# Splitting float64 weights in place, two chunks at a time, without GpSimd

## The chip, the core and the metric

The kernel runs on one core of one Trainium2 chip, as a single launch. The metric is the device time in microseconds, the median of several runs. The engines of a core are TensorE (PE in the rows; its weight loads are PEld), VectorE (DVE), ScalarE (ACT), GpSimd (POOL) and SyncE (SP), whose queue issues all the loads and stores of this kernel.

## What is computed

Three blocks follow one another: a small two-way attention between 512 tokens and 32 state rows per head, a gated feed-forward block with a convolution over three positions, and a second feed-forward block with a squared ReLU and a gate.

```python
# x: (8, 8, 512, 64), state: (8, 8, 32, 64), float32
a = softmax(scale * x @ state.T);  xread = a @ state
a2 = softmax(scale * state @ x.T); sread = a2 @ x
x = concatenate([xread, sread], axis=2)        # per batch: 544 tokens of 512 features
h = maximum(x @ w_in, 0)                       # w_in: 512 x 1024
conv = sum over k of conv_w[k] * h[token + k - 1]
x = (h * sigmoid(conv)) @ w_out                # w_out: 1024 x 512
prev = x of the token before
k = maximum((mu_k * x + (1 - mu_k) * prev) @ w_k, 0)     # w_k: 512 x 1024
r = sigmoid((mu_r * x + (1 - mu_r) * prev) @ w_r)        # w_r: 512 x 512
out = r * ((k * k) @ w_v)                      # w_v: 1024 x 512
```

The five weight matrices and conv_w come as float64.

## The kernel before

Every float32 product runs as three float32r passes: an operand is split into hi, its upper 12 significant bits, and lo, the rest, and hi*hi, hi*lo and lo*hi are accumulated (`mm3`, L112 to L114). So every weight has to be split on the chip before it is used.

A matrix comes in chunks of 128 x 512 entries: 8 of w_in, 8 of w_out, 8 of w_k, 8 of w_v and 4 of w_r, 36 in all. `Weights.load` loads a chunk twice, as two transfers of 512 KB: `raw` holds the 64 bits of each entry as two words, `mid` the same bits shifted by 16, so that one word has the lower part of the mantissa. `Weights.split` makes hi and lo of a chunk: ScalarE takes the magnitude (L156) and the sign (L162) of the upper words into the working tiles `val` and `exp`; VectorE clamps the exponent (L158) and shifts it to its place (L159); GpSimd multiplies by the sign, which is hi (L163); VectorE takes the exponent of hi (L164) and the lower bits of `mid` (L167). The low product is one VectorE instruction (L171) for w_in and w_v, and a ScalarE copy (L173) with a GpSimd product (L174) for w_out, w_k and w_r. `raw` and `mid` have three slots each, `val` and `exp` two each. The slots of `raw` serve the tiles of `pair_m` as well.

Phase 1 has nine tiles: eight batches of 512 positions, and one that gathers the positions whose convolution needs the state's read. A tile has eight slots of 128 hidden features. In a slot TensorE makes h (hps), ScalarE and VectorE make the convolution (L444, L446) and the gate (L454, L456), the gated h is split (L462, L464), and TensorE accumulates the product with w_out (acc). In the first three tiles the low part of the gated h (L464) is GpSimd's, and in the first tile the gating (L456) too. The read of the attention is not formed: h = relu(a m) with m = state w_in, made per batch (`Attention.m`) or for two batches together (`pair_m`). Phase 2 runs over tiles of 384 and then 512 tokens: the mixes with the previous token (L534 to L542), k (kps), its square and split (L557 to L571), r (rps) and the product with w_v.

The order of work is a list of half-slots. `at_half(k, ...)` says at which half-slot a step is written down and with what priority; a scheduler then lays out each engine's fixed order by priority and its own estimate of times. `weight_at(w, need, at)` places a chunk's load and split by the half-slot that needs it. w_in and w_out are split during the first tile, w_k, w_v and w_r during the last tiles of phase 1 and the first of phase 2.

Of the kernel before, what the change touches and what calls it, by code (L numbers as in the profile page):

```python
# [23 lines left out]
# Half-slots of a tile at which the next batch's attention starts, and from a batch's first  # L24
# half-slot those at which the parts of state w_in are made.
# [5 lines left out]
def tile_kernel(  # L31
# [76 lines left out]
    def mm3(ps, lhs, rhs, start, stop):  # L108
        """lhs, rhs: lists over the contraction of (hi, lo)."""
        last = len(lhs) - 1  # L110
        for k, ((lh, ll), (rh, rl)) in enumerate(zip(lhs, rhs)):
            nc.tensor.matmul(ps, lh, rh, start=start and k == 0, stop=False)  # L112
            nc.tensor.matmul(ps, lh, rl, start=False, stop=False)  # L113
            nc.tensor.matmul(ps, ll, rh, start=False, stop=stop and k == last)  # L114

    # ---------------------------------------------------------------- weights
    class Weights:
        """A [P, n] array in DRAM as its (hi, lo); float64 comes as its bits, in an integer type."""

        def __init__(self, src, n, pool, tag=""):  # L120
            self.src, self.n, self.pool, self.tag = src, n, pool, tag
            self.wide = src.dtype != F32

        def tile(self, shape, dt, name, bufs):
            return self.pool.tile(shape, dt, tag=name + self.tag, name=name, bufs=1 if self.tag else bufs)

        def load(self):
            if not self.wide:
                self.raw = self.tile([P, self.n], F32, "raw", 3)
                nc.sync.dma_start(out=self.raw, in_=self.src)  # L130
# [5 lines left out]
            nc.sync.dma_start(  # L136
                out=self.mid.rearrange("p n two -> p (n two)").bitcast(U16)[:, :n],
                in_=self.src.bitcast(U16)[:, 1:1 + n],
            )

        def split(self, w, eng):
            """w[:, 0] + w[:, 1] is the value, to float32's precision or better.

            float64: the exponent is clamped to float32's range and moved to its place; with the sign
            and the upper 11 bits of the mantissa it is hi. The next 25 bits, as a number, times the
            power of two is lo; the load that is off by 16 bits has them in one word."""
            hi, lo = w[:, 0], w[:, 1]
            if not self.wide:
                nc.scalar.activation(hi, self.raw, AF.Copy)
                eng.tensor_tensor(lo, self.raw, hi.bitcast(F32), op=ALU.subtract)  # L150
# [11 lines left out]
            nc.scalar.activation(ef, high.bitcast(F32), AF.Sign)  # L162
            nc.gpsimd.tensor_tensor(hi, vf, ef, op=ALU.mult)  # L163
# [3 lines left out]
            nc.vector.tensor_scalar(  # L167
                v, self.mid[:, :, 0], scalar1=0x1FFFFFF, scalar2=None, op0=ALU.bitwise_and
            )
# [8 lines left out]
    def weight(src, key, tag, pool, eng, many=1):  # L178
        """The two steps in which chunk `key` of a matrix gets ready."""
        r = Weights(src, N, stg)  # L180

        def split():
            name, k = key
            if k % many == 0:
                W[name, "group", k // many] = pool.tile(
                    [P, 2, many, N], F32R, tag=f"{tag}{k // many}", name=f"{name}{k}"
                )
            W[key] = W[name, "group", k // many][:, :, k % many]
            r.split(W[key], eng)

        return r.load, split

    # ---------------------------------------------------------------- attention
# [28 lines left out]
    def pair_m(b, q, g):  # L222
        """state w_in of both batches, for the q-th pair of column blocks and the heads of group g.

        Its rows come out by batch and then head; the copies between partitions put each batch's
        rows together."""
# [7 lines left out]
        r = stg.tile([P, 2, 2, 2 * P], F32R, tag="raw", name="m", bufs=3)  # L234
# [7 lines left out]
    class Attention:  # L242
# [9 lines left out]
        def state(self):  # L252
            """The batch's state^T, with the heads of a group side by side."""
# [9 lines left out]
        def m(self, q, f0, n):  # L263
            """state w_in for the column blocks f0.. f0 + n of the q-th pair of them."""
# [545 lines left out]
```

## Time and profile before

| | before |
|---|---|
| median of 3 runs | 915.64 us (915.46 to 915.88) |
| span of the profiled execution, first to last instruction | 912.2 us |
| TensorE busy (4440 matmuls) | 858.1 us, 94% |
| VectorE busy | 589.2 us, 65% |
| ScalarE busy | 543.4 us, 60% |
| GpSimd busy | 195.1 us, 21% |
| mean granted TensorE clock | 0.976 of full speed |

The time of the profiled execution itself isn't listed beside its span; the runs lie 3.4 us above the span. The shares are means over the whole span; the stages differ, and the rows below are taken by stretch. In the rows a duration in the groups is a mean in ns, and "idle before" is the time that the engine waited in front of the group.

### The profile page before, as it was taken

The page shows a single profiled execution, that of the slowest core. Times are in us where ns is not written, and L with a number is a line of the kernel's source. Part 1 is how long each engine was busy: PE and PEld are TensorE (multiplying, and loading weights), DVE is VectorE, ACT ScalarE, POOL GpSimd, SP SyncE. Part 2 cuts the span into 40 slices and gives each one's busy share as a digit, 9 for nine tenths or more (in the row PEclk, how much of TensorE's full clock was granted, in tenths as well). Part 3 has the DMA queues.
Part 4 walks back from the last instruction along what each step waited for, and adds up shares of the span by engine and source line. Part 5 has one row for each costly group of instructions (what it writes and reads, how often), then busy time and mean ns, then how long its engine had stood idle before and what let it go on. Part 6 is the DMA issues. An engine that isn't in the chain of part 4 may idle for free.

```text
span 912.2 us, 12185 instructions
## 1 busy us (share of the span) xinstructions
PE 858.1 (94%) x4440; PEld 693.0 (76%) x4440; DVE 589.2 (65%) x1001; ACT 543.4 (60%) x985; POOL 195.1 (21%) x280
## 2 busy tenths in 40 slices
PE   4877999999999998998879999999999999999997
PEld 2565677778778876788758888888888888888886
DVE  6999998799889978999895542533435234232221
ACT  4666686678558758777666753645546354553431
POOL 3567754242111113436530000000000000000000
PEclk7778999999999999999999999999999999999999
DMA  9944335534443437426832011111011110011010
GB/s 346 323 160 153 124 131 139 155 111 133 158 126 115 116 94 233 163 83 225 287 108 81 19 29 46 47 47 44 4 47 47 47 47 17 30 35 47 0 47 35
DMA packets 50843, 95.77 MB, mean 105 GB/s; under 512 B 9056, under 2 KB 31072, under 8 KB 48736
## 3 DMA queue, kind: packets, MB, share of 16 engines
q1 hardware_dynamic: 50784, 95.00, 32.1%
q8 instruction: 35, 0.57, 0.3%
q14 instruction: 24, 0.20, 0.1%
HBM read 64.54 MB, written 17.86 MB: 90 GB/s over the span
## 4 chain that ended last, share of the span: by engine, by line
PE 66%; DVE 22%; ACT 4%; DMA 3%; issue 2%; SPq 1%; POOL 1%; DVEq 0%; ACTq 0%; POOLq 0%
PE acc L113 10%; PE acc L114 10%; PE acc L112 10%; PE kps L112 6%; PE kps L113 6%; PE kps L114 6%; DVE cacc L446 5%; PE rps L113 3%; PE rps L114 3%; PE rps L112 3%; DVE val L167 2%; DVE exp L164 2%; DVE val L159 2%; PE hps L112 2%; DVE g L456 2%
## 5 line engine op out<-in xcount | busy, mean ns | idle before, releaser
L571 DVE TENSOR_TENSOR ks<-k,ks 128x512 fp32r<-128x512 f32 (+1 forms) x72 | 48.6, 676 | 116.7 <-ACT ks L570 116.1
L446 DVE SCALAR_TENSOR_TENSOR cacc<-hb,vcol,cacc 128x512 f32<-128x512 f32 (+1 forms) x144 | 112.2, 790 | 4.1 <-ACT cacc L444 3.7
L112 PE MATMUL kps<-xk,k 128*128 128x512 f32 (+1 forms) x288 | 110.6, 384 | 3.7 <-ACT xk L541 3.0
L113 PE MATMUL acc<-gs,out 128*128 128x512 f32 (+1 forms) x288 | 111.4, 387 | 1.8 <-DVE gs L464 1.8
L114 PE MATMUL acc<-gs,out 128*128 128x512 f32 (+1 forms) x288 | 108.0, 386 | 2.8 <-POOL out L174 2.8
L113 PE MATMUL kps<-xk,k 128*128 128x512 f32 (+1 forms) x288 | 110.1, 382 | 0.0
L114 PE MATMUL kps<-xk,k 128*128 128x512 f32 (+1 forms) x288 | 110.0, 382 | 0.0
L112 PE MATMUL acc<-v,ks 128*128 128x512 f32 x272 | 105.9, 393 | 2.8 <-ACT ks L570 1.4
L113 PE MATMUL acc<-v,ks 128*128 128x512 f32 x272 | 105.9, 390 | 0.4 <-DVE v L171 0.4
L114 PE MATMUL acc<-v,ks 128*128 128x512 f32 x272 | 105.1, 392 | 0.0
L112 PE MATMUL acc<-gs,out 128*128 128x512 f32 (+1 forms) x288 | 100.0, 388 | 3.0 <-POOL out L163 2.2
L536 DVE SCALAR_TENSOR_TENSOR mix<-yt,muc,mix 128x384 f32<-128x384 f32 (+7 forms) x128 | 66.6, 542 | 49.4 <-ACT mix L534 48.8
L534 ACT ACTIVATE mix<-yt,om 128x384 f32<-128x384 f32 (+7 forms) x128 | 61.4, 516 | 39.0 <-DMA yt<-y 20.3
L570 ACT ACTIVATE ks<-k 128x512 fp32r<-128x512 f32 (+1 forms) x72 | 43.4, 604 | 67.1 <-PE acc L114 66.9
L557 ACT ACTIVATE k<-kps 128x512 f32<-128x512 f32 (+1 forms) x72 | 40.7, 567 | 48.4 <-PE kps L114 48.0
L113 PEld LDWEIGHTS acc<-gs,out 128*128 128x128 f32 x288 | 55.1, 191 | 15.1 <-DVE gs L464 2.5
L112 PEld LDWEIGHTS acc<-gs,out 128*128 128x128 f32 x288 | 55.0, 192 | 15.1 <-POOL out L163 3.0
L114 PEld LDWEIGHTS acc<-gs,out 128*128 128x128 f32 x288 | 54.6, 191 | 14.4 <-POOL out L174 2.9
L112 PEld LDWEIGHTS kps<-xk,k 128*128 128x128 f32 x288 | 54.2, 188 | 14.9 <-ACT xk L541 3.4
L113 PEld LDWEIGHTS kps<-xk,k 128*128 128x128 f32 x288 | 54.4, 189 | 10.2
L114 PEld LDWEIGHTS kps<-xk,k 128*128 128x128 f32 x288 | 54.3, 189 | 10.2
L112 PEld LDWEIGHTS acc<-v,ks 128*128 128x128 f32 x272 | 50.9, 188 | 14.3 <-POOL v L163 2.0
(134 smaller groups left out, 1882.5 us busy)
## 6 DMA issues: line engine op xcount, KB each, us to landing
out<-r SPq DMA_DIRECT2D x34, 256.0 KB, 2.1
xT<-x_t SPq DMA_DIRECT2D x32, 256.0 KB, 4.1
xn<-x_n SPq DMA_DIRECT2D x8, 1024.0 KB, 5.9
y<-yo SPq DMA_DIRECT2D x8, 1024.0 KB, 4.3
me<-m SPq DMA_DIRECT2D x48, 128.0 KB, 2.4
m_odd<-m SPq DMA_DIRECT2D x48, 128.0 KB, 2.4
raw<-w_in SPq DMA_DIRECT2D x8, 512.0 KB, 5.8
raw<-w_out SPq DMA_DIRECT2D x8, 512.0 KB, 4.8
```

The costliest lines, as they stand in the source:

```text
L112: nc.tensor.matmul(ps, lh, rh, start=start and k == 0, stop=False)
L113: nc.tensor.matmul(ps, lh, rl, start=False, stop=False)
L114: nc.tensor.matmul(ps, ll, rh, start=False, stop=stop and k == last)
L159: nc.vector.tensor_scalar(v, v, scalar1=3, scalar2=0xFFFFF000, op0=ALU.logical_shift_left, op1=ALU.bitwise_and)
L164: nc.vector.tensor_scalar(e, hi.bitcast(U32), scalar1=0xFF800000, scalar2=None, op0=ALU.bitwise_and)
L167: nc.vector.tensor_scalar(v, self.mid[:, :, 0], scalar1=0x1FFFFFF, scalar2=None, op0=ALU.bitwise_and)
L446: nc.vector.scalar_tensor_tensor(a[:, :n], hb[:, k:k + n], w[k], a[:, :n], op0=ALU.mult, op1=ALU.add)
L534: nc.scalar.activation(tmp[:, o:o + m], y[:, c, q - 1:q - 1 + m], AF.Copy, scale=om[:, i:i + 1])
L536: nc.vector.scalar_tensor_tensor(tmp[:, o:o + m], y[:, c, q:q + m], muc[:, i:i + 1], tmp[:, o:o + m], op0=ALU.mult, op1=ALU.add,)
L557: nc.scalar.activation(k[:, :n], s["p"][:, :n], AF.Relu)
L570: nc.scalar.activation(ks[:, 0, :n], s["k2"][:, :n], AF.Copy)
L571: nc.vector.tensor_tensor(ks[:, 1, :n], s["k2"][:, :n], ks[:, 0, :n].bitcast(F32), op=ALU.subtract)
```

## The change

A `Weights` object now stands for `many` chunks of a matrix (two for all five matrices, one for conv_w), loaded by one pair of transfers for each chunk into one slot for all of them. `raw` and `mid` have two slots of two chunks. The split works on both chunks in one instruction per step and in place: the magnitude and then the shifted value take the place of the lower word in `raw`, the sign and then the exponent that of the upper word, and the masked bits stay in `mid`; `val` and `exp` are gone. Both products are VectorE's, for all matrices. The tiles of `pair_m` take the slots of `raw` for the heads of group 0 and those of `mid` for group 1. The places of the loads and splits in the list of half-slots are set anew, and the prologue loads and splits two chunks of w_in and two of w_out instead of two and one. Comment lines are gone as well.

```diff
+        def __init__(self, src, many, n, pool, tag=""):
+            self.src, self.many, self.n, self.pool, self.tag = src, many, n, pool, tag
...
-            self.raw = self.tile([P, self.n, 2], U32, "raw", 3)
-            nc.sync.dma_start(out=self.raw.rearrange("p n two -> p (n two)"), in_=self.src.bitcast(U32))
-            self.mid = self.tile([P, self.n, 2], U32, "mid", 3)
+            self.raw = self.tile([P, self.many, self.n, 2], U32, "raw")
+            self.mid = self.tile([P, self.many, self.n, 2], U32, "mid")
             n = 4 * self.n - 2
...
+            for i, src in enumerate(self.src):
+                nc.sync.dma_start(out=self.raw[:, i].rearrange("p n two -> p (n two)"), in_=src.bitcast(U32))
+                nc.sync.dma_start(
+                    out=self.mid[:, i].rearrange("p n two -> p (n two)").bitcast(U16)[:, :n],
+                    in_=src.bitcast(U16)[:, 1:1 + n],
+                )
...
-            high = self.raw[:, :, 1]
-            v = self.tile([P, self.n], U32, "val", 2)
-            e = self.tile([P, self.n], U32, "exp", 2)
+            v, e, m = self.raw[:, :, :, 0], self.raw[:, :, :, 1], self.mid[:, :, :, 0]
             vf, ef = v.bitcast(F32), e.bitcast(F32)
-            nc.scalar.activation(vf, high.bitcast(F32), AF.Abs, scale=2.0**16)
+            nc.scalar.activation(vf, ef, AF.Abs, scale=2.0**16)
...
-            nc.scalar.activation(ef, high.bitcast(F32), AF.Sign)
-            nc.gpsimd.tensor_tensor(hi, vf, ef, op=ALU.mult)
+            nc.scalar.activation(ef, ef, AF.Sign)
+            nc.vector.tensor_tensor(hi, vf, ef, op=ALU.mult)
...
-            nc.vector.tensor_scalar(
-                v, self.mid[:, :, 0], scalar1=0x1FFFFFF, scalar2=None, op0=ALU.bitwise_and
-            )
-            if eng is nc.vector:
-                nc.vector.scalar_tensor_tensor(lo, v, 2.0**-36, ef, op0=ALU.mult, op1=ALU.mult)
-            else:
-                nc.scalar.activation(vf, v, AF.Copy, scale=2.0**-36)
-                eng.tensor_tensor(lo, vf, ef, op=ALU.mult)
+            nc.vector.tensor_scalar(m, m, scalar1=0x1FFFFFF, scalar2=None, op0=ALU.bitwise_and)
+            nc.vector.scalar_tensor_tensor(lo, m, 2.0**-36, ef, op0=ALU.mult, op1=ALU.mult)
...
-        r = stg.tile([P, 2, 2, 2 * P], F32R, tag="raw", name="m", bufs=3)
+        r = stg.tile([P, 2, 2, 2 * P], F32R, tag=("raw", "mid")[g], name="m", bufs=2)
...
-        if f > 1:
-            weight_at(win[f], 2 * f - 1, 2 * f - 3)
+        if f % 2 == 0:
+            weight_at(win[f // 2], 2 * f - 1, max(0, 2 * f - 5))
...
-    for f in range(1, KF):
-        weight_at(wout[f], 2 * f + 5, 2 * f + 3)
+    for f in range(2, KF, 2):
+        weight_at(wout[f // 2], 2 * f + 5, 2 * f + 2)
...
-                    weight_at(w, h, h - 3)
+                    weight_at(w, h, h - 4)
...
-                    weight_at(w, h + 1, h - 2)
+                    weight_at(w, h + 1, h - 3)
...
-                    weight_at(w, h, h - 1)
+                    weight_at(w, h, h - 2)
```

## Rows read from the trace of the kernel before

**Rows 1.** The page: the span, and each engine's busy time.

```profile
span 912.2 us, 12185 instructions
PE 858.1 (94%) x4440; PEld 693.0 (76%) x4440; DVE 589.2 (65%) x1001; ACT 543.4 (60%) x985; POOL 195.1 (21%) x280
```

**Rows 2.** Busy us by stretch: window, length, PE, PEld, DVE, ACT, POOL, clock, DMA.

```profile
0.00:125.00 125.00, 93.91 (x534) 69.16 (x535) 113.72 (x189) 77.46 (x138) 75.75 (x90) 0.82 0.61 213
125.00:340.00 215.00, 212.83 (x1340) 168.81 (x1339) 187.94 (x325) 149.93 (x256) 57.60 (x113) 1.00 0.43 127
340.00:480.00 140.00, 123.85 (x691) 103.00 (x690) 130.87 (x219) 102.30 (x199) 61.14 (x71) 1.00 0.56 182
```

**Rows 3.** Busy us by stretch on tile val alone: DVE, ACT, POOL.

```profile
0.00:125.00 125.00, 47.07 (x60) 15.95 (x25) 35.29 (x25) 0.82 0.61 213
340.00:480.00 140.00, 35.61 (x68) 20.81 (x32) 50.29 (x32) 1.00 0.56 182
```

**Rows 4.** Busy us by stretch of line L164 alone: DVE.

```profile
0.00:125.00 125.00, 11.29 (x17) 0.82 0.61 213
340.00:480.00 140.00, 14.89 (x20) 1.00 0.56 182
```

**Rows 5.** Timeline of all engines, 0 to 30 us: start, us, instruction.

```profile
28.53 1.55 POOL L163 TENSOR_TENSOR in<-val,exp 128x512 fp32r<-128x512 f32 x1 [0.89 <-ACT val L156]
...
28.96 1.40 DVE L159 TENSOR_SCALAR val<-val 128x512 uint32<-128x512 uint32 x1
```

**Rows 6.** Instructions on tile val: ns at minimum, median, maximum.

```profile
L159 DVE TENSOR_SCALAR val<-val x37: 162/419/1503, 11.7 to 473.3; 128x512 uint32<-128x512 uint32 x36, 128x24 uint32<-128x24 uint32 x1
L167 DVE TENSOR_SCALAR val<-mid x37: 166/414/1532, 15.0 to 477.5; 128x512 uint32<-128x512 uint32 x36, 128x24 uint32<-128x24 uint32 x1
...
L171 DVE SCALAR_TENSOR_TENSOR in<-val,exp x8: 617/931/1768, 16.5 to 84.6; 128x512 fp32r<-128x512 uint32 x8
```

**Rows 7.** Groups of instructions on POOL, 0 to 125 us.

```profile
L464 POOL TENSOR_TENSOR gs<-g,gs 128x512 fp32r<-128x512 f32 x10 | 15.1, 1513 | 1.7 <-ACT gs L462 1.7
...
L456 POOL TENSOR_TENSOR g<-g,hb 128x512 f32<-128x512 f32 x8 | 9.9, 1240 | 1.7 <-ACT g L454 1.7
```

**Rows 8.** Groups of instructions on DVE, 0 to 125 us.

```profile
L446 DVE SCALAR_TENSOR_TENSOR cacc<-hb,vcol,cacc 128x512 f32<-128x512 f32 x24 | 20.8, 878 | 0.1
```

**Rows 9.** Groups on DVE, shapes apart, 250 to 340 us.

```profile
L446 DVE SCALAR_TENSOR_TENSOR cacc<-hb,vcol,cacc 128x512 f32<-128x512 f32 x32 | 23.4, 741 | 0.7 <-ACT cacc L444 0.6
```

**Rows 10.** Groups on DVE, shapes apart, 340 to 480 us.

```profile
L446 DVE SCALAR_TENSOR_TENSOR cacc<-hb,vcol,cacc 128x512 f32<-128x512 f32 x24 | 19.6, 828 | 0.1
...
L456 DVE TENSOR_TENSOR g<-g,hb 128x512 f32<-128x512 f32 x12 | 11.4, 954 | 0.0
...
L536 DVE SCALAR_TENSOR_TENSOR mix<-yt,muc,mix 128x384 f32<-128x384 f32 x8 | 6.9, 866 | 0.0
...
L542 DVE TENSOR_TENSOR xk<-mix,xk 128x512 fp32r<-128x512 f32 x4 | 3.8, 956 | 0.1
```

**Rows 11.** Groups on DVE, shapes apart, 480 to 912 us.

```profile
L542 DVE TENSOR_TENSOR xk<-mix,xk 128x512 fp32r<-128x512 f32 x24 | 16.6, 692 | 10.3 <-ACT xk L541 10.1
...
L536 DVE SCALAR_TENSOR_TENSOR mix<-yt,muc,mix 128x384 f32<-128x384 f32 x8 | 4.9, 618 | 4.4 <-ACT mix L534 4.3
```

**Rows 12.** Busy us by stretch as in rows 2, first 24 us; last: GB/s.

```profile
0.00:24.00 24.00, 10.63 (x41) 6.38 (x42) 16.93 (x41) 9.71 (x21) 9.08 (x20) 0.74 0.95 348
```

**Rows 13.** Waits of SyncE's queue, 24 to 125 us: total, times, longest.

```profile
SPq L136 <- DVE val L167: 53.3, 11, 15.3
```

**Rows 14.** DMA issues: count, size, median us to landing.

```profile
raw<-w_in SPq DMA_DIRECT2D x8, 512.0 KB, 5.8
```

**Rows 15.** Timeline of POOL, 24 to 125 us: the last weight product.

```profile
114.13 1.29 POOL L174 TENSOR_TENSOR out<-val,exp 128x512 fp32r<-128x512 f32 x1 [1.04 <-ACT val L173]
```

**Rows 16.** Timeline of SyncE's queue.

```profile
345.98 2.21 SPq L133 DMA_DIRECT2D raw<-w_k  x3
```

More of the change, by code (lines that the diff above doesn't have):

```diff
@@ L117, in tile_kernel, with tile, split @@
     class Weights:
[L120 to L125, printed above, removed]
+        def __init__(self, src, many, n, pool, tag=""):
+            self.src, self.many, self.n, self.pool, self.tag = src, many, n, pool, tag
+            self.wide = src[0].dtype != F32
+        def tile(self, shape, dt, name):
+            return self.pool.tile(shape, dt, tag=name + self.tag, name=name, bufs=1 if self.tag else 2)
         def load(self):
             if not self.wide:
-                self.raw = self.tile([P, self.n], F32, "raw", 3)
-                nc.sync.dma_start(out=self.raw, in_=self.src)
+                self.raw = self.tile([P, self.many, self.n], F32, "raw")
+                for i, src in enumerate(self.src):
+                    nc.sync.dma_start(out=self.raw[:, i], in_=src)
                 return
-            self.raw = self.tile([P, self.n, 2], U32, "raw", 3)
-            nc.sync.dma_start(out=self.raw.rearrange("p n two -> p (n two)"), in_=self.src.bitcast(U32))
-            self.mid = self.tile([P, self.n, 2], U32, "mid", 3)
+            self.raw = self.tile([P, self.many, self.n, 2], U32, "raw")
+            self.mid = self.tile([P, self.many, self.n, 2], U32, "mid")
             n = 4 * self.n - 2
-            nc.sync.dma_start(
-                out=self.mid.rearrange("p n two -> p (n two)").bitcast(U16)[:, :n],
-                in_=self.src.bitcast(U16)[:, 1:1 + n],
-            )
-        def split(self, w, eng):
+            for i, src in enumerate(self.src):
+                nc.sync.dma_start(out=self.raw[:, i].rearrange("p n two -> p (n two)"), in_=src.bitcast(U32))
[3 more added lines that the diff above has]
+                )
+        def split(self, w):
             hi, lo = w[:, 0], w[:, 1]
@@ L166, in split, with weight @@
             )
-            nc.vector.tensor_scalar(
-                v, self.mid[:, :, 0], scalar1=0x1FFFFFF, scalar2=None, op0=ALU.bitwise_and
-            )
-            if eng is nc.vector:
-                nc.vector.scalar_tensor_tensor(lo, v, 2.0**-36, ef, op0=ALU.mult, op1=ALU.mult)
-            else:
-                nc.scalar.activation(vf, v, AF.Copy, scale=2.0**-36)
-                eng.tensor_tensor(lo, vf, ef, op=ALU.mult)
+            nc.vector.tensor_scalar(m, m, scalar1=0x1FFFFFF, scalar2=None, op0=ALU.bitwise_and)
+            nc.vector.scalar_tensor_tensor(lo, m, 2.0**-36, ef, op0=ALU.mult, op1=ALU.mult)
     W = {}
-    def weight(src, key, tag, pool, eng, many=1):
-        r = Weights(src, N, stg)
+    def weight(src, key, tag, pool, k, many, group):
+        r = Weights([src[k + i] for i in range(many)], many, N, stg)
         def split():
[L183 to L189, printed above, removed]
+            g = (key, "group", k // group)
+            if k % group == 0:
+                W[g] = pool.tile([P, 2, group, N], F32R, tag=f"{tag}{k // group}", name=f"{key}{k}")
+            o = k % group
+            for i in range(many):
+                W[key, k + i] = W[g][:, :, o + i]
+            r.split(W[g][:, :, o:o + many])
         return r.load, split
@@ L610, in run_half @@
             fn()
-    win = [weight(w_in[f], ("in", f), "wa", wp, nc.vector, 4) for f in range(KF)]
-    wout = [weight(w_out[f], ("out", f), "wb", wp, nc.gpsimd) for f in range(KF)]
-    vec = Weights(conv, 3 * KF, const, "c")
+    win = [weight(w_in, "in", "wa", wp, 2 * i, 2, 4) for i in range(KF // 2)]
+    wout = [weight(w_out, "out", "wb", wp, 2 * i, 2, 2) for i in range(KF // 2)]
+    vec = Weights([conv], 1, 3 * KF, const, "c")
     vs = const.tile([P, 2, 3 * KF], F32R, name="vs")
@@ L621, in tile_kernel @@
     nc.sync.dma_start(out=muc, in_=mu)
-    win[1][0]()
     wout[0][0]()
@@ L644, in tile_kernel @@
         a.turn1(g)
-    vec.split(vs, nc.vector)
+    vec.split(vs.rearrange("p l (o n) -> p l o n", o=1))
     nc.vector.tensor_tensor(vcol, vs[:, 0].bitcast(F32), vs[:, 1].bitcast(F32), op=ALU.add)
     nc.vector.tensor_scalar(om, muc, scalar1=-1.0, scalar2=1.0, op0=ALU.mult, op1=ALU.add)
-    win[1][1]()
     wout[0][1]()
@@ L714, in tile_kernel @@
                 p2 = ctx.enter_context(tc.tile_pool(name="p2", bufs=1))
-                for k in range(KF):
-                    w = weight(w_k[k], ("k", k), "wk", p2, nc.gpsimd)
+                for k in range(0, KF, 2):
+                    w = weight(w_k, "k", "wk", p2, k, 2, 2)
                     h = h2 + 2 * k
-                    weight_at(w, h, h - 3)
-                for k in range(KF):
-                    w = weight(w_v[k], ("v", k), "wa", wp, nc.vector, 4)
+                    weight_at(w, h, h - 4)
+                for k in range(0, KF, 2):
+                    w = weight(w_v, "v", "wa", wp, k, 2, 4)
                     h = h2 + 2 * k + 4
-                    weight_at(w, h + 1, h - 2)
-                for k in range(KC):
-                    w = weight(w_r[k], ("r", k), "wb", wp, nc.gpsimd)
+                    weight_at(w, h + 1, h - 3)
+                for k in range(0, KC, 2):
+                    w = weight(w_r, "r", "wb", wp, k, 2, 2)
                     h = h2 + 8
-                    weight_at(w, h, h - 1)
+                    weight_at(w, h, h - 2)
                 at_half(2 * i + 4, lambda: load_y(0, p2))
```

2 lines of the change are left out of this document (1 added, 1 removed).

## The prediction

> **What bounds the kernel now.** The span is 912.2 us, the median of the runs 915.64, so about 3.4 us lie around the span; sums below are made against the span and 3.4 is added at the end. A measurement of this kernel tells 0.2% (1.8 us) from no change. I read the busy times of the page first [rows 1]: TensorE is busy for 858.1 us, so at most 54 us can be won by keeping it fed. The busy times by stretch say where those 54 us lie [rows 2]. From 125 to 340 TensorE has 212.8 of 215 us: nothing to win there. In the first 125 us it is busy for 93.9, at a mean granted clock of 0.82 between its levels of 1.2 and 2.4 GHz, while VectorE is busy for 113.7; with the first 24 us and their 16.9 [rows 12] set aside, in which the first loads arrive, that is 96.8 of 101. From 340 to 480, where the weights of phase 2 are split, TensorE has 123.9 of 140 and is idle for 16.2, and VectorE has 130.9. The weight splits fall into exactly these two stretches and nowhere else, so VectorE sets the pace where the change acts.
>
> What does VectorE do there? The instructions on the split's working tile, together with L164 (which does not write that tile), give the split's time on VectorE: 47.07 + 11.29 = 58.4 us in the first stretch and 35.61 + 14.89 = 50.5 in the second [rows 3, 4]. Most of it is not arithmetic. One tensor_scalar of 512 columns takes 414 ns at the median and 1,532 at worst [rows 6], and the timeline shows when [rows 5]: GpSimd's product begins at 28.53 and runs to 30.08, and the tensor_scalar that starts at 28.96 takes 1.40 us, to 30.36; it is held until GpSimd is done. So every product on GpSimd is paid for on VectorE as well.
>
> The Trainium skill, page "SBUF — State Buffer", section "Who interferes with whom", puts it as an exclusive lock: a VectorE instruction with two SBUF inputs, or in a two-port mode, contends with a GpSimd instruction that reads SBUF, and the loser waits for the whole instruction. The trace agrees, by those 1.40 us against 0.414.
>
> **The change, part by part: VectorE's own work.** A chunk now costs four tensor_scalars, and where the low product is VectorE's, an L171 as well. Without waits that is 4 x 0.414 = 1.66 and 0.617 [rows 6]. For the 16 chunks of the first stretch: 64 x 0.414 + 8 x 0.617 = 31.4. The convolution's vector of 24 columns costs 5 x 0.17 = 0.9. The rest, 58.4 - 0.9 - 31.4 = 26.1, is waiting.
>
> After the change a pair costs four tensor_scalars and two products, of 1,024 columns. A tensor_scalar takes 166 ns for 24 columns and 414 for 512 [rows 6], 0.51 ns a column, so 414 + 260 = 674 ns for 1,024. A product of 1,024 columns has no row: it is bounded by twice 617 = 1,234 and by that less one fixed part of 166, 1,068; I take 1,150, in the middle. A pair is 4 x 0.674 + 2 x 1.15 = 5.0 us; eight pairs 40.0, ten pairs 50.0. VectorE thus takes over the products at 40.0 - 31.4 = 8.6 us more own work in the first stretch.
>
> **The waiting that goes.** Of the work on GpSimd with two inputs in the first stretch, the weights hold 35.3 us [rows 3]; the low part of the gated h (L464, 15.1) and the gating (L456, 9.9) stay [rows 7]. Besides the 26.1 us on the split, the convolution's 24 instructions wait: 878 ns against 741 in a stretch with little on GpSimd, 3.3 us [rows 8, 9]. That is 29.4 us of waiting for 60.3 us on GpSimd, 0.49 each. If the 25.0 us that stay go on costing 0.49, 12.2 are left. VectorE's sum goes from 31.4 + 29.4 = 60.8 to 40.0 + 12.2 = 52.2, which is -8.6. The bounds: if what stays costs nothing, -20.8; if VectorE, now with longer instructions, waits as long as before, +8.6. I take -8.6, by the row's own ratio. VectorE is busy for 96% of this stretch after the prologue, so it counts one for one.
>
> In the second stretch the 50.5 us become 50.0, with next to nothing left on GpSimd with two inputs; the 50.3 us of weight products there go [rows 3]. The work beside the split gains: in groups of 512 columns L456 takes 954 ns and L542 956 against 692 alone, L446 828 against 741, L536 of 384 columns 866 against 618 [rows 9, 10, 11]: 12 x 0.262 + 4 x 0.264 + 24 x 0.087 + 8 x 0.248 = 8.3 us. So VectorE loses 8.8 us of 130.9. TensorE can follow only as far as it idles, 16.2 us [rows 2]. Bounds: 0 and -16.2; I take the middle, -8.1, near VectorE's own 8.8.
>
> **Costed at nothing, and what hides it.** ScalarE's 25 and 32 instructions on the working tile take 15.95 and 20.81 us, 0.64 each [rows 3]; Abs and Sign become half as many, at most twice as long, and the copies of L173 go, so its sum falls. It is busy for 77.5 of 125 and 102.3 of 140 us [rows 2] and has room; without that room the first instruction of a pair would start VectorE's part 0.64 us later, eight times in the first stretch. The staging memory stays the same size (three slots of one chunk each for the high and the middle words, and two for each working tile, become two slots of two chunks). The prologue's first split needs the high words of two chunks, 1 MB more behind the first; at 348 GB/s [rows 12] that is up to 3 us later, but the second chunk is then done too, and the two waits on GpSimd in that chain go; I put it at 0, with 3 us as the upper end. The loads keep their number and bytes, but SyncE's queue changes: from 24 to 125 us it stood still for 53.3 us in front of the second load of a chunk until L167 had freed a slot [rows 13]. It now waits once for four loads, with the loads of x and of the state's tiles behind it; the pair_m tiles use both staging tags, so the first loads of w_k stay behind the last of these.
>
> **The sum.** 912.2 - 8.6 - 8.1 = 895.5, and 3.4 around it: 899 us.
>
> **The rivals.**
> *Only the first stretch gains.* TensorE's 16.2 idle us in the second may be those of the hand-over between the phases, whose chain of loads and mixes the change leaves alone. 912.2 - 8.6 + 3.4 = 907.
> *Nothing is left.* The longer instructions of VectorE and what stays on GpSimd hold each other up as much as before (the bound of +8.6 in the first stretch, against -8.1 in the second): 916.
>
> *The slots become the bound, and it gets slower.* Values, exponents and low words now sit in the loaded buffers, so a slot is held from the load to the last product; before, it was free after Sign or after L167. The place is SyncE's queue in front of the next pair. A pair needs a load of four transfers: the first lands after 5.8 us [rows 14] and three of 0.5 MB follow at 348 GB/s, 1.5 us each, about 10 us; then at most 1.3 on ScalarE and 5.0 on VectorE, which I double to about 12 since VectorE has other work. That is 22 us a turn. In the first stretch each slot must make three more turns after 24 us, and the last low product is done at 115.4 now [rows 15]: slower only from (115.4 - 24)/3 = 30 us a turn. In the second, ten pairs on two slots are five turns; from 346 us, when SyncE issues the first load of w_k [rows 16], to 480 that allows 26.8 us a turn. At 28.5 us a turn phase 2's weights would be 8.5 us late and the first stretch would win nothing: 924. Against it stands the distance from 22 to 26.8; for it, that a static order cannot mend a late load, and all that is queued behind it on ScalarE and VectorE waits with it.
>
> *Writing in place with a step of two words loses the fast rate.* Reading with that step costs nothing: L167 reads every second word of the staged tile and takes 414 ns like the contiguous ones [rows 6]. No row writes with it. At one column per 1.04 ns (half the rate) a tensor_scalar would take 1.22 us: 0.55 x 32 = 17.6 us more in the first stretch and 22 in the second, of which some is hidden: about 935. The Trainium skill, page "VectorE: DVE Perf Modes", section "What auto-detection actually checks", asks for one source and a destination in SBUF and an even outermost count, not for a step of one; by that rule this case does not happen, and no run here shows a write of this kind.
>
> **Chances and range.** The forecast 0.57, only the first stretch 0.15, nothing left 0.07, the slots 0.13, the step 0.05, and 0.03 for a TensorE that follows all the way (912.2 - 20.8 - 16.2 + 3.4 = 879). Faster: 0.57 + 0.15 + 0.03 = 0.75; same 0.07; slower 0.18. The range from 885 to 922 leaves out the far gain, the step and the worse half of the slots, and a little of the forecast's tail. The forecast's own range is 888 to 908.
>
> **What would show it.** VectorE's tensor_scalars of 1,024 columns at about 0.67 us and products at 1.15; no weight product on GpSimd; VectorE busy about 105 us in the work that took 113.7; the last product of w_out before 110 us; TensorE's idle time between 340 and 480 halved. I am wrong if a pair costs VectorE more than 7 us, if ScalarE's Abs waits for loads by more than some 10 us in total, or if TensorE's idle time stays although VectorE's falls.

## The result, and the profile after

The kernel after takes 899.07 us (897.87 to 901.15), the kernel before, run beside it, 915.55: a ratio of 0.9825, 95% interval 0.9808 to 0.9842. The forecast was 899. The spans of the two profiled executions differ by 13.0 us (912.2 to 899.2, [rows 1]) and the medians by 16.5, because the execution profiled after is 2.1 us slower than its median (901.15) and the one before, whose time isn't listed, some 1.5 faster than its own, as every execution with both numbers on record takes 1.7 to 2.1 us more than its span and not 3.4. So in which part of the kernel 3.5 of the 16.5 us were won, the two traces do not show. L numbers in this section are those of the kernel after (magnitude L158, clamp and shift L160 and L161, sign L164, hi L165, exponent L166, mask L169, lo L170, loads L138 and L139).

The page of the kernel after, span and busy times; against [rows 1] GpSimd has lost 76 us and VectorE 25:

```profile
span 899.2 us, 12003 instructions
PE 850.8 (95%) x4440; PEld 692.3 (77%) x4440; DVE 564.0 (63%) x950; ACT 531.2 (59%) x929; POOL 118.8 (13%) x223
```

Busy us by stretch of the kernel after (window, length, PE, PEld, DVE, ACT, POOL, clock, DMA), against [rows 2]:

```profile
0.00:125.00 125.00, 92.21 (x551) 70.24 (x552) 108.84 (x172) 77.03 (x123) 47.46 (x70) 0.84 0.56 209
125.00:340.00 215.00, 209.54 (x1322) 165.16 (x1321) 183.44 (x320) 146.20 (x247) 53.81 (x110) 1.00 0.44 127
340.00:480.00 140.00, 134.50 (x748) 115.43 (x747) 122.31 (x204) 103.11 (x185) 16.90 (x39) 0.99 0.54 191
```

The forecast was -8.6 us from the first stretch and -8.1 from the second. In the second TensorE's idle time fell from 16.2 to 5.5 us. In the first it is busy for 92.2 us where it was 93.9, at a mean clock of 0.84 where it was 0.82, and gets further: 551 matmuls where it was 534. Two markers say what became of that, the first store of y and the fifth, the latter in the stretch in which TensorE is nearly full (timeline of SyncE's queue, before and then after):

```profile
124.62 0.33 SPq L484 DMA_DIRECT2D y<-yo  x1
...
290.85 0.33 SPq L484 DMA_DIRECT2D y<-yo  x1
```
```profile
119.76 0.33 SPq L481 DMA_DIRECT2D y<-yo  x1
...
290.91 0.33 SPq L481 DMA_DIRECT2D y<-yo  x1
```

At the first store the change is 4.9 us ahead, with 528 matmuls done where it was 532; at the fifth, with 1,572 done in both, it is not. What it had won was lost in between: from 125 to 340 us TensorE's idle time rose from 2.2 to 5.5. Its two longest waits there are for the copies of m:

```profile
138.28 0.47 PE L112 MATMUL hps<-aring,me 128*128 128x512 f32 x1 [1.55 <-DMA me<-m]
...
177.25 0.47 PE L112 MATMUL hps<-aring,me 128*128 128x512 f32 x1 [1.53 <-DMA me<-m]
```

The marker itself is good to some 2 us: e3_pool2 below has the same order of instructions as the change up to the fifth store, and issues it at 288.89. So up to there 0 to 2 us were won, and 11 to 13 come later: 912.2 - 290.85 = 621.4 us become 899.2 - 290.91 = 608.3. The total was right by luck: one term was too large and the other too small by about as much.

**Where the second stretch won.** The windows narrowed to the end of that stretch, before and then after:

```profile
400.00:480.00 80.00, 67.66 (x365) 57.76 (x364) 74.77 (x130) 54.22 (x113) 38.08 (x33) 1.00 0.59 191
```
```profile
400.00:480.00 80.00, 79.78 (x436) 71.46 (x435) 68.61 (x120) 57.53 (x111) 4.40 (x11) 1.00 0.55 201
```

Here TensorE idled for 12.3 us and idles for 0.2 now: 12.1 of the 13. VectorE's groups in the kernel after, 325 to 480 us (busy us, mean ns, idle before and what ended it):

```profile
L443 DVE SCALAR_TENSOR_TENSOR cacc<-hb,vcol,cacc 128x512 f32<-128x512 f32 x24 | 17.6, 744 | 1.8 <-ACT cacc L441 1.7
L453 DVE TENSOR_TENSOR g<-g,hb 128x512 f32<-128x512 f32 x12 | 8.2, 686 | 1.3 <-ACT g L451 1.3
L160 DVE TENSOR_SCALAR raw<-raw 128x1024 f32<-128x1024 f32 x10 | 6.9, 694 | 3.9 <-ACT raw L158 3.5 <-DMA m_odd<-m 0.3
...
L533 DVE SCALAR_TENSOR_TENSOR mix<-yt,muc,mix 128x384 f32<-128x384 f32 x8 | 4.9, 615 | 0.0
L170 DVE SCALAR_TENSOR_TENSOR k<-mid,raw 128x1024 fp32r<-128x1024 uint32 x4 | 4.9, 1220 | 0.0
```

A tensor_scalar of 1,024 columns takes 0.69 us (forecast 0.674) and a product 1.22 (forecast 1.15): 4 x 0.69 + 2 x 1.22 = 5.2 a pair instead of 5.0. The neighbours fall as forecast, L453 from 954 to 686 and the mix from 866 to 615 [rows 10].

**Where the first stretch did not.** The same split of the window into four, of which the first 24 us were 10.63 before [rows 12]; the other three before, then all four after:

```profile
24.00:60.00 36.00, 27.88 (x171) 19.31 (x171) 35.30 (x64) 25.51 (x43) 21.57 (x22) 0.74 0.79 275
60.00:90.00 30.00, 23.38 (x179) 19.17 (x179) 29.87 (x38) 19.64 (x37) 21.29 (x22) 0.90 0.40 135
90.00:125.00 35.00, 32.02 (x146) 24.30 (x146) 31.62 (x49) 22.60 (x38) 23.82 (x27) 0.90 0.36 124
```
```profile
0.00:24.00 24.00, 8.71 (x30) 3.79 (x31) 16.17 (x35) 10.12 (x19) 5.55 (x16) 0.78 0.95 343
24.00:60.00 36.00, 21.94 (x154) 15.89 (x153) 32.20 (x45) 19.35 (x26) 8.66 (x11) 0.78 0.73 283
60.00:90.00 30.00, 26.64 (x137) 22.82 (x138) 29.89 (x47) 21.54 (x34) 10.88 (x11) 0.75 0.39 145
90.00:125.00 35.00, 34.93 (x234) 27.73 (x233) 30.58 (x48) 26.01 (x47) 22.38 (x33) 1.00 0.27 95
```

From 60 us on TensorE gains 6.2 us of busy time, but before 60 it loses 7.9. Its longest waits in the kernel after (timeline of PE; the bracket is the wait and what ended it):

```profile
17.63 0.69 PE L112 MATMUL p_m<-in,aux 128*128 128x128 f32 x2 [8.00 <-DVE in L165]
...
60.75 0.69 PE L380 MATMUL p_srT<-ident,sr 128*128 128x128 f32 x2 [8.38 <-ACT e L315]
```

The last one can be followed back. ScalarE's timeline, and then SyncE's:

```profile
48.96 1.14 ACT L158 ACTIVATE raw<-raw 128x1024 f32<-128x1024 f32 x1 [4.29 <-DMA raw<-w_out]
...
57.48 1.13 ACT L158 ACTIVATE raw<-raw 128x1024 f32<-128x1024 f32 x1 [3.72 <-DVE cacc L443]
...
59.92 0.69 ACT L315 ACTIVATE e<-p_s,s 128x512 f32<-128x512 f32 x1
```
```profile
21.46 0.33 SPq L138 DMA_DIRECT2D raw<-w_in  x1
...
41.92 0.33 SPq L138 DMA_DIRECT2D raw<-w_out  x1
...
60.69 0.33 SPq L138 DMA_DIRECT2D raw<-w_out  x1
```

(These three are loads into the same slot of raw, 20.5 and 18.8 us apart; into the other slot they are 19.5 and 21.5 apart.) The exponentials that TensorE waits for stand on ScalarE behind two magnitudes of a pair. The first waits 4.3 us for a load that SyncE issued only at 41.92. The second is put down to VectorE's convolution, which had long been done; its pair's loads were issued at 49.0 to 50.4 in the same timeline, so it too is a load (the second of its two transfers into raw lands at 57.38). SyncE's waits, 0 to 125 us, show what held the loads (against [rows 13], where it was the mask L167):

```profile
SPq L204 <- PE p_sr L363: 24.2, 2, 23.3
SPq L138 <- DVE in L170: 18.5, 2, 10.6
...
SPq L138 <- DVE out L170: 10.8, 2, 6.2
```

A pair's buffer comes free with L170, the last instruction of the split. The first row, L204, held no weight: its 23.3 us begin behind the last load of phase 1's weights.

VectorE's own account in this stretch came out as forecast:

```profile
L443 DVE SCALAR_TENSOR_TENSOR cacc<-hb,vcol,cacc 128x512 f32<-128x512 f32 x26 | 26.2, 1023 | 6.7 <-ACT cacc L441 6.5
L161 DVE TENSOR_SCALAR raw<-raw 128x1024 uint32<-128x1024 uint32 x8 | 6.5, 817 | 0.0
L160 DVE TENSOR_SCALAR raw<-raw 128x1024 f32<-128x1024 f32 x8 | 6.4, 799 | 0.5 <-ACT raw L158 0.5
L170 DVE SCALAR_TENSOR_TENSOR in<-mid,raw 128x1024 fp32r<-128x1024 uint32 x4 | 5.9, 1466 | 0.0
L169 DVE TENSOR_SCALAR mid<-mid 128x1024 uint32<-128x1024 uint32 x8 | 5.8, 719 | 0.0
L170 DVE SCALAR_TENSOR_TENSOR out<-mid,raw 128x1024 fp32r<-128x1024 uint32 x4 | 5.7, 1429 | 0.0
L165 DVE TENSOR_TENSOR in<-raw 128x1024 fp32r<-128x1024 f32 x4 | 4.9, 1222 | 0.6 <-DVE raw L161 0.5
L165 DVE TENSOR_TENSOR out<-raw 128x1024 fp32r<-128x1024 f32 x4 | 4.8, 1210 | 0.0
```

With L166 (2.7 + 2.7) the split takes 45.4 us. Eight pairs at 5.2 are 41.6, so 3.8 of it is waiting; the convolution waits 26 x (1.023 - 0.741) = 7.3. That makes 41.6 + 11.1 = 52.7 us, where 52.2 were forecast. The 11.1 us of waiting stand where 12.2 were expected for the work left on GpSimd.

But the time did not follow VectorE. Up to the fifth store TensorE has done the same 1,572 matmuls in the following three versions. The busy times up to there (columns as in [rows 2]), before, after, and in e1_vec, which moves the products alone (below):

```profile
0.00:290.85 290.85, 257.59 (x1572) 198.37 (x1573) 256.98 (x436) 195.37 (x340) 124.81 (x182) 0.92 0.51 165
```
```profile
0.00:290.91 290.91, 252.67 (x1572) 195.85 (x1573) 247.58 (x413) 191.20 (x316) 92.73 (x157) 0.93 0.49 160
```
```profile
0.00:282.70 282.70, 252.92 (x1572) 193.94 (x1573) 253.84 (x461) 192.74 (x332) 93.12 (x157) 0.95 0.51 170
```

The change took 9.4 us from VectorE and won 0 to 2; e1_vec took 3.1 and won 8.2.

### The profile page after: what moved, and what is told of

It is laid out like the page before. It is cut to its first block, busy times and chain, and to the rows that moved or that the text cites. A ratio compares the mean times of both kernels' runs of the same rounds, so it can differ in the third digit from the quotient of the medians.

```text
span 899.2 us, 12003 instructions
## 1 busy us (share of the span) xinstructions
PE 850.8 (95%) x4440; PEld 692.3 (77%) x4440; DVE 564.0 (63%) x950; ACT 531.2 (59%) x929; POOL 118.8 (13%) x223
## 4 chain that ended last, share of the span: by engine, by line
PE 83%; DVE 8%; ACT 3%; issue 2%; DMA 2%; POOL 1%; SPq 0%; DVEq 0%; ACTq 0%; POOLq 0%
PE acc L113 13%; PE acc L114 13%; PE acc L112 13%; PE kps L112 7%; PE kps L113 7%; PE kps L114 7%; PE rps L114 3%; PE rps L113 3%; PE rps L112 3%; PE hps L112 3%; PE hps L114 3%; PE hps L113 3%; DVE cacc L443 2%; PE p_s L284 2%; PE p_m L113 1%
## 5 line engine op out<-in xcount | busy, mean ns | idle before, releaser
L113 PE MATMUL acc<-gs,out 128*128 128x512 f32 (+1 forms) x288 | 110.6, 386 | 0.0
L114 PE MATMUL acc<-gs,out 128*128 128x512 f32 (+1 forms) x288 | 109.6, 384 | 0.0
L112 PE MATMUL acc<-gs,out 128*128 128x512 f32 (+1 forms) x288 | 94.3, 389 | 4.3 <-ACT gs L459 4.3
L533 DVE SCALAR_TENSOR_TENSOR mix<-yt,muc,mix 128x384 f32<-128x384 f32 (+7 forms) x128 | 61.1, 500 | 47.7 <-ACT mix L531 47.2
L112 PEld LDWEIGHTS acc<-gs,out 128*128 128x128 f32 x288 | 53.7, 192 | 16.1 <-ACT gs L459 6.1
L113 PEld LDWEIGHTS acc<-gs,out 128*128 128x128 f32 x288 | 54.8, 190 | 12.8 <-POOL hb L429 0.8
L113 PEld LDWEIGHTS kps<-xk,k 128*128 128x128 f32 x288 | 54.4, 189 | 10.1
L114 PEld LDWEIGHTS kps<-xk,k 128*128 128x128 f32 x288 | 54.3, 188 | 10.1
L451 ACT ACTIVATE g<-cacc 128x512 f32<-128x512 f32 (+1 forms) x72 | 43.8, 609 | 27.5 <-DVE cacc L443 19.4
```

Source lines behind the costliest of these rows:

```text
L451: nc.scalar.activation(g[:, :n], s["a"][:, :n], AF.Sigmoid)
L533: nc.vector.scalar_tensor_tensor(tmp[:, o:o + m], y[:, c, q:q + m], muc[:, i:i + 1], tmp[:, o:o + m], op0=ALU.mult, op1=ALU.add,)
```

## The experiments

Every version was timed against the kernel before. In the table "up to y" is the start of the fifth store of y in the profiled execution less 290.85, and "after y" the rest of the span less 621.4, so each says what a version won (negative) in the first part and in the second. Both columns are of one execution each, and good to some 2 us (the first columns of the change and of e3_pool2 are the same work).

| version | us | ratio and interval | up to y | after y |
|---|---|---|---|---|
| the change | 899.07 | 0.9825 [0.9808, 0.9842] | +0.1 | -13.1 |
| e1_vec | 890.98 | 0.9736 [0.9720, 0.9751] | -8.2 | -15.4 |
| e2_pool1 | 914.59 | 0.9994 [0.9982, 1.0005] | +9.6 | -10.2 |
| e3_pool2 | 913.29 | 0.9984 [0.9967, 1.0000] | -2.0 | -0.3 |
| e4_half0 | 901.86 | 0.9861 [0.9837, 0.9886] | -0.4 | -12.0 |
| e5_halves | 902.13 | 0.9851 [0.9833, 0.9868] | -0.4 | -10.6 |
| e6_inplace4 | 901.88 | 0.9854 [0.9836, 0.9871] | -3.1 | -10.1 |
| e7_slots2 | 892.52 | 0.9754 [0.9738, 0.9769] | -8.7 | -13.1 |
| e8_gate | 890.32 | 0.9726 [0.9711, 0.9741] | -8.5 | -15.3 |
| r9_mid | 892.81 | 0.9758 [0.9743, 0.9772] | -5.9 | -16.1 |
| r10_raw | 897.52 | 0.9808 [0.9792, 0.9825] | -2.5 | -13.5 |
| r12_w1500 | 893.31 | 0.9764 [0.9749, 0.9778] | -6.2 | -15.1 |
| r13_w2000 | 898.98 | 0.9824 [0.9809, 0.9839] | -3.8 | -10.7 |

### The products alone, or the rebuilding alone

**e1_vec**: the kernel before, chunk by chunk and not in place, with both products on VectorE.

```diff
-            nc.gpsimd.tensor_tensor(hi, vf, ef, op=ALU.mult)
+            nc.vector.tensor_tensor(hi, vf, ef, op=ALU.mult)
...
-            if eng is nc.vector:
-                nc.vector.scalar_tensor_tensor(lo, v, 2.0**-36, ef, ...)
-            else: ...
+            nc.vector.scalar_tensor_tensor(lo, v, 2.0**-36, ef, ...)
```

> The kernel before with one thing changed: all hi and lo products of the weights on VectorE, still chunk by chunk, nothing in place. Theory A (the gain of the change is VectorE no longer being held by GpSimd's products; the pairs only make the moved work cheap): VectorE's own split work rises to 64 x 0.414 + 32 x 0.617 = 46.2 us in the first stretch and 80 x 0.414 + 40 x 0.678 = 60.2 in the second, the waiting goes; part of the gain, 905 to 912. Theory B (the gain is that of fewer, longer instructions on pairs, whoever does the products): no pairs, more work on VectorE, so no gain or a loss, 915 to 925.

890.98 us, 8 less than the change and far below both expectations. The two lines are worth 24 us by themselves; everything else in the change takes 8 of them back, and by the table's columns (8.3 and 2.3 us) mostly in the first part.

**e2_pool1** and **e3_pool2** put products of the change back on GpSimd, as pairs: e2 those of phase 1 (hi of w_in, hi and lo of w_out), e3 those of phase 2 (hi of w_k, w_v and w_r, lo of w_k and w_r).

```diff
-            nc.vector.tensor_tensor(hi, vf, ef, op=ALU.mult)
+            (nc.gpsimd if key in HIS else nc.vector).tensor_tensor(hi, vf, ef, op=ALU.mult)
...
+            if key in LOS:
+                nc.scalar.activation(mf, m, AF.Copy, scale=2.0**-36)
+                nc.gpsimd.tensor_tensor(lo, mf, ef, op=ALU.mult)
```

> The changed kernel with the products of w_in and w_out back where they were (hi of both and lo of w_out on GpSimd, as pairs), phase 2's left on VectorE. Theory A with the first stretch worth what was forecast (8.6 us): 904 to 908, and the tensor_scalars of 1,024 columns in the first 125 us rise from about 0.75 to 1.5 us or more. If the first stretch gave nothing to the end, as the equal stores of y at 248 to 329 us in both kernels suggest: 898 to 901. Theory B: 899.

> The changed kernel with the products of w_k, w_v and w_r back where they were (hi of all and lo of w_k and w_r on GpSimd, as pairs), phase 1's left on VectorE. Theory A: the gain of the second stretch is lost, 908 to 914, with TensorE idle for 12 us or more between 340 and 480. Theory B (pairs alone): 899 to 902, TensorE idle there for about 6 us.

Each gives nearly the whole gain back, at the place where the products stand: e2 loses 9.5 us in the first part, e3 12.8 in the second. For e3 that is as theory A had it; e2's 914.59 is above all that was expected, and the sign named for it did not come: its tensor_scalars of 1,024 columns take 0.68 to 1.18 us on average in the first 125, not 1.5 or more. In e2's groups on GpSimd, 0 to 125 us, one product of a pair takes 1.9 to 2.9 us, and its timeline of PE shows TensorE waiting for them and for the lo that follows (L175):

```profile
L173 POOL TENSOR_TENSOR out<-mid,raw 128x1024 fp32r<-128x1024 f32 x4 | 11.8, 2948 | 3.7 <-DVE raw L166 3.7
...
L165 POOL TENSOR_TENSOR in<-raw 128x1024 fp32r<-128x1024 f32 x4 | 7.6, 1894 | 15.7 <-DMA mid<-w_out 10.7 <-ACT raw L164 2.2 <-DVE raw L161 1.5
```
```profile
18.12 0.69 PE L112 MATMUL p_m<-in,aux 128*128 128x128 f32 x2 [8.84 <-POOL in L165]
25.75 0.48 PE L113 MATMUL p_m<-in,aux 128*128 128x128 f32 x1 [6.93 <-DVE in L175]
```

In e3 TensorE idles for 6.8 us of the window from 400 to 480, where the change idles for 0.2:

```profile
400.00:480.00 80.00, 73.19 (x400) 64.32 (x400) 65.80 (x101) 53.93 (x104) 30.83 (x23) 1.00 0.50 181
```

So the gain is the products' place, in both stretches. The pairs bring none of it: with the products on GpSimd, the rebuilt kernel is 9.6 us behind the kernel before in the first part (e2) and even with it in the second (e3).

What GpSimd's products cost is not VectorE's time alone. The 1,078 matmuls behind the fifth store, before and then in e3:

```profile
290.85:500.00 209.15, 193.00 (x1078) 158.83 (x1077) 185.86 (x316) 146.35 (x277) 69.78 (x93) 1.00 0.50 159
```
```profile
288.89:497.80 208.91, 194.10 (x1078) 160.18 (x1077) 176.93 (x271) 142.92 (x250) 68.26 (x77) 0.99 0.49 167
```

VectorE is busy for 8.9 us less, and 0.2 us are won. The other way in which a product on GpSimd can cost time is as a step between a chunk's load and TensorE, as in e2's waits above; no run sets the two apart.

### What takes 8 us back

**e4_half0**: the change, with only the first pair of w_in split chunk by chunk (its first hi is there earlier). **e5_halves**: the same for every pair, with the change's two slots of two chunks.

```diff
+            parts = [slice(i, i + 1) for i in range(self.many)] if halves else [slice(0, self.many)]
+            for s in parts:
...
-            r.split(W[g][:, :, o:o + many])
+            r.split(W[g][:, :, o:o + many], (key, k) == ("in", 0))      # e5: True
```

> The changed kernel with the first pair of w_in alone split chunk by chunk (same slot, same engines, twice the instructions of half the size), so that the first product for m can begin after one chunk. If the later start of TensorE (first hi at 17.6 us against 13.6) is what ate the first stretch's gain: 895 to 897. If later waits in the first tile set its end (TensorE idle for 4.7 us until 36.7 and 8.4 until 60.8): 898 to 901.

> The changed kernel with every pair split chunk by chunk: twice the instructions of 512 columns, on the same two slots of two chunks, in place, at the same places in the list. Theory P (the long instructions on a pair are what costs the 8 us against products on VectorE alone, 891): 891 to 895, although VectorE's own work rises by some 8 us in the first stretch. Theory S (the slots are what costs: two chunks are loaded, held to the last product and freed together): 898 to 903.

Neither gains: 901.86 us is near what was expected if later waits count, 902.13 is as theory S has it. In e4 TensorE's first weight is ready at 14.59 us instead of 17.63, and the time comes back as waits further on (9.0 us at 38.48 and 8.1 at 61.51). A late prologue is not what the first stretch lost, and neither is the length of the instructions.

**e7_slots2**: e1_vec with two slots of one chunk for raw and mid instead of three. **e6_inplace4**: e1_vec split in place, chunk by chunk, with four slots and without val and exp.

```diff
-            self.raw = self.tile([P, self.n, 2], U32, "raw", 3)
+            self.raw = self.tile([P, self.n, 2], U32, "raw", 2)         # e6: 4; mid the same
...
-            v = self.tile([P, self.n], U32, "val", 2)                   # e6 alone
-            e = self.tile([P, self.n], U32, "exp", 2)
+            v, e, m = self.raw[:, :, 0], self.raw[:, :, 1], self.mid[:, :, 0]
```

> The kernel before with all products on VectorE, and two slots of one chunk for raw and mid in place of three (val and exp unchanged). Theory S (slots and late loads set the first tiles' pace): 896 to 910. Theory P: 890 to 894.

> The kernel before with all products on VectorE and split in place, chunk by chunk, in four slots of one chunk each for raw and mid (the same memory as the pairs). Theory P: 888 to 893, as there are no pairs. Theory S: if it is holding a slot to the last product that costs, 895 to 900; if it is that two chunks are loaded and freed together, 888 to 893.

Two slots for three cost 1.5 us, which is within what a measurement of this kernel can tell. Splitting in place, with more slots than before, costs 10.9, without any pair; that is above what either theory expected, and nearest to a slot held to the last product.

**r9_mid** and **r10_raw** take e6 apart, with three slots: r9 keeps only the masked bits in mid, r10 only value and sign in raw. **r12_w1500** changes nothing but the fixed order. **r13_w2000** is e6 with its loads and splits laid out earlier.

```diff
-                v, self.mid[:, :, 0], scalar1=0x1FFFFFF, ...
+                self.mid[:, :, 0], self.mid[:, :, 0], scalar1=0x1FFFFFF, ...    # r9
...
-            v = self.tile([P, self.n], U32, "val", 2)                            # r10
-            e = self.tile([P, self.n], U32, "exp", 2)
+            v, e = self.raw[:, :, 0], self.raw[:, :, 1]
+            m = self.tile([P, self.n], U32, "val", 2)
...
-AHEAD, M_AHEAD, EXP_AHEAD, WEIGHT_AHEAD = 1500, 2000, 50000, 1000
+AHEAD, M_AHEAD, EXP_AHEAD, WEIGHT_AHEAD = 1500, 2000, 50000, 1500               # r12; r13: e6 with 2000
```

> This is the kernel with the chunk-by-chunk split and all products on VectorE (890.98 us) with one thing more: the masked lower bits stay in mid, so mid is held until the low product (VectorE's last instruction of the split) and no longer only until the mask; raw is still free after the sign. Theory H (a buffer held longer makes the next load start later, and the split's fixed order then waits for the load): mid is held only by about one product longer (0.7 to 1.5 us a chunk), raw not at all, so little is lost: 891 to 895 us, and ScalarE's magnitude waits for loads under 3 us in the second stretch, as it did with nothing held (0.9 us). Theory O (the loss comes from another fixed order of TensorE's work, not from the buffers): its order of TensorE's matmuls is displaced in the second stretch as that of the in-place version was (a mean of 9.7 places there, 13.6 in the in-place version), so about 897 to 902 us.

> The same base (890.98 us), with value and sign now in place in raw, so raw is held from its load to the low product, three slots as in the base; the masked bits go to a tile of their own, so mid is free after the mask. Theory H: raw is held some 3 us longer in every chunk, which is most of what the in-place version did, and with three slots instead of four: 897 to 903 us, with ScalarE's magnitude waiting 5 us or more for loads in the second stretch. Theory O: the order is displaced little in the second stretch (2.4 places), so 890 to 893 us.

> The same base (890.98 us) with nothing changed but the weight steps' priority (500 higher), which alters the fixed order a little (TensorE's by a mean of 3.0 places among the first 500 matmuls and 0.6 among those of the second stretch). It shows how much the time moves by order alone. Theory H: within 2 us of the base, 889 to 893 us. Theory O: 4 us or more to either side.

> The in-place version with single chunks and four slots (901.88 us) with the weight steps' priority raised by 1000, so that loads and splits are laid out earlier where the list lets them. Theory H: the loads still wait for the buffers, which the low product releases, so 898 to 904 us. Theory L (in place costs only because its steps stand too late in the fixed order): most of the 11 us comes back, 891 to 895 us.

Against e1_vec, mid held costs 1.8 us and raw held 6.5, while another order alone costs 2.3. So r10's loss is the one that stands clear of what that one other order does, and r9's is not told from it. How far TensorE's order is displaced does not decide: r9, with the larger displacement in the second stretch, loses nothing there (0.7 us less than e1_vec), r10, hardly displaced there, 1.9, both near what a column is good to. Most of r10's loss, 5.7 us, lies in the first part; there, counted from the traces, e1_vec's first 500 matmuls are displaced by a mean of 5 places in r10, and by 8 in r9 and e8, which lose less or nothing. That another order of the same extent could cost as much is not shown to be out. Raising the priority brings 2.9 of e6's 10.9 us back, little more than the order alone moved, so lateness in the fixed order is at most the smaller part. Of the expectations on time, r9's, r10's and r13's theory H came true; r12's 893.31 is at its edge.

What a held buffer does is seen in SyncE's waits from 325 to 480 us, in e1_vec and then in r10_raw (L133 is the load of raw there):

```profile
SPq L133 <- ACT exp L162: 32.4, 11, 5.8
```
```profile
SPq L133 <- DVE k L170: 33.1, 7, 9.9
```

In e1_vec the load follows ScalarE's sign, in r10 VectorE's last product. ScalarE's magnitude in the same stretch, e1_vec, then r10_raw, then r9_mid:

```profile
L156 ACT ACTIVATE val<-raw 128x512 f32<-128x512 f32 x20 | 13.4, 672 | 0.9 <-DVE k L170 0.6 <-DVE r L170 0.3
```
```profile
L156 ACT ACTIVATE raw<-raw 128x512 f32<-128x512 f32 x20 | 13.5, 675 | 5.0 <-DMA raw<-w_v 2.6 <-DMA raw<-w_k 2.2
```
```profile
L156 ACT ACTIVATE val<-raw 128x512 f32<-128x512 f32 x20 | 13.4, 672 | 7.2 <-DMA raw<-w_v 3.5 <-DMA raw<-w_r 2.1 <-DVE k L163 1.6
```

r10's wait is as expected (5 us or more), but r9's is a miss: of its 7.2 us 5.6 are put down to loads, and under 3 were expected. ScalarE's wait does not say what a version costs: r9 has the longest of the three and wins most after y, and in the first 125 us, where r10 loses most, ScalarE stands idle in front of the magnitude for 10.3 us in r10 and 12.9 in e1_vec.

### A version that beats both

**e8_gate**: e1_vec, and the gating and the first tile's low part (both of phase 1) moved from GpSimd to VectorE too.

```diff
-LOW_ON_POOL = (0, 1, 2)
-GATE_ON_POOL = (0,)
+LOW_ON_POOL = (1, 2)
+GATE_ON_POOL = ()
```

> The kernel before with all products on VectorE, and the gating and the low part of the gated h of the first tile on VectorE too. If VectorE's waiting for GpSimd counts in the first tile (about 17 us there with the products moved, against 16 x 0.68 = 11 us more own work): 886 to 890. If own work counts as much as waiting: 891 to 897.

890.32 us, between the two expectations and the fastest here, but 0.7 under e1_vec, from another set of runs, is within what a measurement of this kernel can tell. In the first stretch its shift takes 471 ns where e1_vec's takes 529, and its convolution 857 where it was 906: VectorE takes over the work and loses about as much waiting.

## Why the prediction was right, and where its steps were not

**VectorE's price of the change: right.** 5.2 us a pair (forecast 5.0), 11.1 us of waiting left (12.2), VectorE's sum of the first stretch 52.7 (52.2), its busy time in the second down by 8.6 (8.8). The gating on VectorE, 954 ns with GpSimd's products beside it and 686 without, shows on one instruction that GpSimd's two-input products were paid for on VectorE. The Trainium skill, page "SBUF — State Buffer", section "Who interferes with whom", lets a two-input VectorE instruction contend with a GpSimd one that reads SBUF; the trace agrees. That removing the products from GpSimd is the gain, e1, e2 and e3 show from both sides.

**First stretch, "it counts one for one": wrong.** This is the step that failed. For the same matmuls up to the fifth store VectorE is busy for 9.4 us less, and 0 to 2 us are won of the 8.6; e1_vec shows that 8.2 were to be had, with 3.1 us less on VectorE. So VectorE's busy time was not what set the pace, or not by itself. The other step is the cost of in-place splitting put at nothing. Its turn was right (22 us forecast, 18.8 to 21.5 measured from load to load), but at that turn ScalarE, which was to have room, waited 8.5 us in front of the magnitudes with the exponentials that TensorE needed behind them. Of e1_vec's 8.2 us single chunks in place keep 3.1 (e6), raw held alone keeps 2.5 (r10), and pairs 0 to 2.

**Second stretch, the middle of TensorE's idle time: too small.** -8.1 forecast, -13.1 measured, and -15.4 without the rebuilding. VectorE's saving was right at 8.6, yet nearly all of TensorE's idle time from 400 to 480 went. The middle between 0 and 16.2 was chosen because it lay near VectorE's own sum; e3, with 8.9 us less on VectorE and 0.2 won, shows that this sum is no measure of it. GpSimd's part in a chunk's chain, which fell away with the products, is the candidate that is left; no run tests it by itself.

**The rivals.** "Only the first stretch gains" has the two stretches exchanged. "Nothing is left" is out: the interval of the ratio ends at 0.9842. "The slots become the bound" came nearest to what eats 8 of the 24 us, a slot held from load to last product and a fixed order that can't mend a late load; it forecast a loss against before, at 28.5 us a turn, and the whole stays faster at turns of 18.8 to 21.5. "Writing in place loses the fast rate" is out: 0.69 us for 1,024 columns, not 1.22. The Trainium skill, page "VectorE: DVE Perf Modes", section "What auto-detection actually checks", asks nothing of the step for 32-bit data with one source, and the trace agrees.

**What would show it.** The last product of w_out was to be done before 110 us; it begins at 90.69. That it came 23 us earlier than [rows 15] and 0 to 2 us were won shows that the end of the splits did not set this part. ScalarE's magnitude was not to wait for loads by more than some 10 us: it waited 4.8 in the first stretch, 3.7 more that are put down to VectorE and end as a load lands, and 5.4 in the second. By that sign, 13.9 us, the forecast's account was wrong, although its number came true.

**What stays open.** Whether GpSimd's products cost by VectorE's waiting or as a step in a chunk's chain, and how a held raw buffer turns into TensorE's lost time. The waits move about between versions (8.4 us at 60.75 in the change, none of over 2.4 us between 36 and 125 in e6), because the scheduler lays out another order for every buffer plan; r10's 6.5 us are the buffer together with the order that follows from it. The one measure of order alone, r12, is 2.3 us. The 3.2 us by which the change stands behind e6 up to y are not assigned, nor is what delays the copies of m behind the first stretch.

## What to carry to other kernels

When two engines hold each other up, moving work to the busier one can pay: in e1_vec VectorE took on (36 + 20) x 0.68 = 38 us of products, and the kernel won 24. An engine that is busy for 96% of a stretch need not set its pace: compare its busy time and the time won for the same work of TensorE. Try such a step alone: the rebuilding around it cost 8. A working tile that lets a load buffer go early can be worth its memory: a buffer that is overwritten in place is held until the last step, the next load starts that much later, and with raw that came to 6.5 us here, together with the fixed order that followed from it.

## What the runs showed of the hardware

- VectorE reads and writes every second word of a buffer at the rate of contiguous words: single chunks in place take 426 ns a tensor_scalar and 688 a product in e6, contiguous ones 418 and 683 in e1_vec (325 to 480 us).
- One VectorE instruction of 1,024 columns is cheaper than two of 512: 0.69 against 2 x 0.42 us, 1.22 against 2 x 0.68. That is 0.9 us a pair; e5_halves, which gives it up for all 18 pairs, takes 3.1 us more than the change, little more than another order alone moved.
- GpSimd's product of 1,024 columns takes 1.9 to 3.1 us (e2, e3), VectorE's 1.22.
